# Two q tiles of batch 1 transposed by DMA instead of TensorE, with the loads of k and v of batch 2 held back and their work moved later

## The chip, the cores and the metric

The kernel runs on one core of one Trainium2 chip. The metric is device time in microseconds (us) of one execution, as the median of several runs; lower is better. The profile comes from one further execution of the same program.

## What is computed

The reference has two parts. The first is a linear attention (cosformer) over q, k and v of shape 8 batches x 8 heads x 576 rows x 64, float32. The second is a gated feed-forward layer over the 4608 rows of 512 that come out of the first.

```python
r = np.maximum(x, 0.0)                                   # phi, for q and for k
phi = np.concatenate([r * cos_w, r * sin_w], axis=-1)    # 64 -> 128 features, angle by row
kv = einsum('bhsf,bhsd->bhfd', k_p, v);  z = sum(k_p, axis=2)
num = einsum('bhsf,bhfd->bhsd', q_p, kv)
x = num / (einsum('bhsf,bhf->bhs', q_p, z)[..., None] + 1e-6)
xn = x / sqrt(mean(x*x) + 1e-6) * rms_g                  # x as 4608 x 512
out = (silu(xn @ w_gate) * (xn @ w_val)) @ w_out         # 512 -> 1536 -> 512
```

## The kernel before

**Blocks.** The output rows are worked on in nine blocks: block b holds the first 512 rows of batch b (for batch 0 another choice of 512 rows), and block 8 the 64 rows left over from each batch. They run in the order 0 to 6, 8, 7. A block has 12 gate steps (n = 0 to 11) and 4 out steps (n = 12 to 15). A gate step (`gval_step`, L869) runs four matmuls with `wg` into a psG bank and four with `wv` into a psV bank (`half_mm`, L556); then ScalarE applies silu to the first bank (`sg`, L570) and VectorE multiplies it with the second into `hT` (L571). psG and psV have two banks each, so the banks of step n are used again in step n + 2. An out step (`out_step`, L894) sums 12 matmuls of `hT` with `wo` in psC (L574); ScalarE copies the bank to `osb`, and the SP queue stores it. Block 0 has its own form of the out steps, `out_first` (L882): 48 matmuls, numbered i = 0 to 47, the first eight of each of four row tiles and then the last four of each.

**What is woven in.** While the matmuls of block b run, batch b + 1 goes through its attention. A table (`at(block, n, where, function, ...)`, L753) says in which step, and where in it, each piece is emitted: "pe" ahead of the step's matmuls, "pre" behind them, "post" at the end of the step. In `out_first` the place can also be a matmul number i. The table sets the order of the instructions on every engine by hand; each engine, and each DMA queue (SP's and GpSimd's), takes its instructions strictly in that order, and waits where an operand is not there.

The pieces of one batch are:

- `load_kv`, `load_q` (L107, L125): 1 MB each for k, v and q into one of five `raw` buffers, from SP's queue, and for the first batches from GpSimd's.
- `k_phi`, `q_phi` (L299, L317): a cosine half on VectorE and a sine half on ScalarE, from `raw` to bf16 `kp` or `qp`. `v_cast` (L369): v to bf16 `vv`.
- `q_tr_dma` (L344): tile j of q (128 rows x 1024) transposed by DMA from SP's queue into `qpT`. `q_tr_pe` with `q_tr_evac` (L359, L365): the same by eight TensorE transposes into a PSUM bank and one copy.
- `kvz_pe`, `kvz_evac` (L382, L442): the state of the batch, 72 small matmuls (40 from batch 3 on) into psA and a copy to `kvzs`. For each pair of heads all k chunks are needed, chunk 8 as the last.
- per row tile j: `nd_pe` (L446), 8 matmuls of `qpT` with `kvzs` into psA; `nd_post` (L507), the division into `xt` on VectorE; `x_sq` (L511), sum of squares on ScalarE and a power on GpSimd (`rs`, L520); `x_norm` (L523), to bf16 `xn` on VectorE; `x_tr_dma` (L539), the transposed tile by DMA from SP into `xnT`. The gate matmuls of a block read all four tiles of its `xnT` at once.

**Around the change.** For batch 1 the q tiles 0 and 1 are transposed by TensorE in steps 10 and 11 of block 0, tile 2 in `last_step` (L796) and tile 3 at i = 9 of `out_first`, each with a copy (VectorE for the first two, ScalarE for the last two). Its row tiles start (`x_first`) at `last_step`, i = 6, 11 and 19. The `xnT` tiles 0 to 2 of batch 1 go by DMA, tile 3 by TensorE at i = 43 (`x_tr`). k and v of batch 2 are loaded from GpSimd's queue in steps 8 and 10 of block 0, and worked on in the steps 14 of block 0 to 1 of block 1; its state is summed in step 3, its row tiles start in the steps 6, 8, 9 and 11 of block 1. k, v and q of batch 3 are loaded in the steps 4, 8 and 12 of block 1 (SP).

Of the kernel before, what the change touches and what calls it, by code (L numbers as in the profile page):

```python
# [10 lines left out]
BF16 = mybir.dt.bfloat16  # L11
# [6 lines left out]
def kernel(  # L18
# [17 lines left out]
    HP = H // 2  # L36
# [10 lines left out]
    V, A, G = nc.vector, nc.scalar, nc.gpsimd  # L47

    ctx.enter_context(tc.manual_schedule())
    one = ctx.enter_context(tc.tile_pool(name="one", bufs=1))  # L50
# [8 lines left out]
    psV = [ps.tile([P, 512], FP32, name=f"psV{i}") for i in range(2)]  # L59
# [10 lines left out]
    def kv_rows(src, b, hps):  # L70
        return src[b, 2 * hps[0] : 2 * hps[1], :, :].rearrange(
            "(hp hh) (s c) d -> (hh s) hp (c d)", hh=2, c=NC
        )

    def wide(b):
        return b > 2
# [4 lines left out]
    def kv_rows5(src, b, r0, r1):  # L81
        part = src[b, :, 0 : NC5 * (KP - 1), :].rearrange(
            "h (p c) d -> p h (c d)", c=NC5
        )[r0 : min(r1, KP - 1)]
        return bass.AP(part.tensor, part.offset, [[NC5 * D, r1 - r0]] + list(part.ap)[1:])
# [12 lines left out]
    def raw_kv(which, b):  # L98
        t = raw_tile(which, b)
        if wide(b):  # L100
            return t[:, :].rearrange("p (h e) -> p h e", h=H)
        return t[:, 0 : HP * NC * D].rearrange("p (hp e) -> p hp e", hp=HP)
# [4 lines left out]
    def load_kv(which, b, hps=(0, HP), eng=nc.sync):  # L107
        src = k if which == "k" else v
        if not wide(b):
            return eng.dma_start(  # L110
                out=raw_kv(which, b)[:, hps[0] : hps[1], :], in_=kv_rows(src, b, hps)
            )
        last = KP if b < B - 1 else KP - 1
        for r0, r1 in ((0, KM), (KM, last)):
            eng.dma_start(
                out=raw_kv(which, b)[r0:r1, :, :], in_=kv_rows5(src, b, r0, r1)
            )
        if last < KP:
            eng.dma_start(
                out=raw_kv(which, b)[last:KP, :, :].rearrange("p h (c d) -> p h c d", d=D),  # L120
                in_=src[b, :, S - 1 : S, :].rearrange("h s d -> s h d").unsqueeze(2)
                .to_broadcast([1, H, NC5, D]),
            )
# [25 lines left out]
    for c0, c1 in ((0, 4), (4, NC)):  # L149
        nc.sync.dma_start(  # L150
            out=raw_kv("k", 0)[:, :, c0 * D : c1 * D],
            in_=kv_rows(k, 0, (0, HP))[:, :, c0 * D : c1 * D],
# [70 lines left out]
    for i in range(3):  # L223
        m, e = math.frexp(left)
# [6 lines left out]
    def g_spread(bank, t):  # L231
# [12 lines left out]
        out=th[:, 0:NTAB], in0=fidx[:, :], scalar1=S - 1.0, scalar2=ang,  # L244
        op0=ALU.min, op1=ALU.mult,
    )
    for c0, c1, i0, less in ((0, 9, 0, 576.0), (13, 14, 13, 64.0), (19, NTAB, 13, 64.0)):
        V.tensor_scalar(
            out=th[64:128, c0:c1], in0=fidx[64:128, i0 : i0 + c1 - c0],
# [4 lines left out]
        out=th[:, NTAB : 2 * NTAB], in0=th[:, 0:NTAB], scalar1=math.pi / 2.0,  # L254
# [4 lines left out]
        out=sel[:, :, :], in_=ident[0:4, 0:4].unsqueeze(2).to_broadcast([4, NDT, P])  # L259
# [30 lines left out]
    def phi(eng, out_ap, in_ap, scale):  # L290
        if eng is A:
            A.activation(out=out_ap, in_=in_ap, func=AF.Relu, scale=scale)  # L292
        else:
            eng.tensor_scalar(  # L294
                out=out_ap, in0=in_ap, scalar1=scale, scalar2=0.0, op0=ALU.mult, op1=ALU.max
            )
# [20 lines left out]
    def q_phi(eng, b, j, part):  # L317
        o = slice(0, D) if part == 0 else slice(D, F)
        f = cos_of if part == 0 else sin_of
        phi(eng, qp_of((b, j))[:, :, o], raw_q(b)[:, :, j * D : (j + 1) * D], f(9 + j))  # L320
# [23 lines left out]
    def q_tr_dma(b, j):  # L344
        t = qp_of((b, j))
        nc.sync.dma_start_transpose(
            out=qpT[:, :, j * P : (j + 1) * P], in_=t[:, :, :].rearrange("p h f -> p (h f)")
        )
# [10 lines left out]
    def q_tr_pe(b, j, bank):  # L359
        t = qp_of((b, j))  # L360
        dst = bank.bitcast(BF16).rearrange("p (h s) -> p h s", h=H)
        for h in range(H):
            nc.tensor.transpose(dst[:, h, :], t[:, h, :], ident[:, :])  # L363

    def q_tr_evac(eng, b, j, bank):  # L365
        dst = bank.bitcast(BF16).rearrange("p (h s) -> p h s", h=H)
        copy(eng, qpT[:, :, j * P : (j + 1) * P], dst)
# [111 lines left out]
    x_of, rs_of, xn_of = {}, {}, {}  # L479
# [84 lines left out]
    def banks_of(blk, n):  # L564
        return psG[n % 2], psV[n % 2]
# [187 lines left out]
    def at(blk, n, where, f, *args):  # L753
        slots.setdefault((blk, n), {}).setdefault(where, []).append((f, args))
# [2 lines left out]
        for f, args in slots.get((blk, n), {}).get(where, []):  # L757
            f(*args)

    KCS = ((0, 1, 2), (3, 4), (5, 6), (7, 8))  # L760
    KCS5 = ((0, 1), (2,), (3,), (4,))
    for c in range(NC):
        at(0, 5 + c // 3, "post", k_phi, V, 1, c, 0)
        at(0, 5 + c // 3, "post", k_phi, A, 1, c, 1)
    for j in range(4):
        at(0, (8, 8, 9, 10)[j], "post", q_phi, V, 1, j, 0)
        at(0, (8, 9, 10, 10)[j], "post", q_phi, A, 1, j, 1)
        bank = (psC[0], psC[1], psV[0], psV[1])[j]
        if j < 2:
            at(0, 10 + j, "pe", q_tr_pe, 1, j, bank)  # L770
            at(0, 10 + j, "pre", q_tr_evac, V, 1, j, bank)
    at(0, 8, "post", load_kv, "k", 2, (0, HP), G)
    at(0, 9, "post", v_cast, G, 1, (0, 2))
    at(0, 10, "pre", v_cast, V, 1, (2, 4))
    at(0, 10, "post", load_kv, "v", 2, (0, HP), G)

    def q_tr(j, bank):
        q_tr_pe(1, j, bank)  # L780
        q_tr_evac(A, 1, j, bank)

    def x_first(j):
        nd_pe(1, j)
# [11 lines left out]
    def last_step():  # L796
        n = NNT - 1
        g, v = banks_of(0, n)
        run(0, n, "pe")
        half_mm(0, n, wg, g)  # L800
        kvz_pe(1)
        sg = four.tile([P, TB], FP32, name="sg", tag="sg")
        A.activation(out=sg[:, :], in_=g[:, 0:TB], func=AF.Silu)
        kvz_evac(A, 1)
        run(0, n, "pre")
        half_mm(0, n, wv, v)
        nd_pe(1, 0)
        q_tr(2, psV[0])
        nd_post(1, 0)
        V.tensor_tensor(out=hT[:, n, :], in0=v[:, 0:TB], in1=sg[:, :], op=ALU.mult)  # L810
        x_sq(1, 0)
        run(0, n, "post")

    for j, i in ((1, 6), (2, 11), (3, 19)):
        at(0, 12, i, x_first, j)
        at(0, 12, i, x_last, j - 1)
    at(0, 12, 9, q_tr, 3, psV[0])
    at(0, 12, 21, x_norm, 1, 3)
    at(0, 12, 21, load_q, 2)
    at(0, 12, 43, x_tr, 3, psV[0])  # L820
    for nb in range(2, B):
        b = nb - 1
        first = nb == 2
        for i, cs in enumerate(KCS5 if wide(nb) else KCS):
            kb, kn = ((0, 14), (0, 15), (1, 0), (1, 1))[i] if first else (b - 1, 12 + i)
            for c in cs:
                at(kb, kn, "post", k_phi, V, nb, c, 0)
                at(kb, kn, "post", k_phi, A, nb, c, 1)
        for i in range(2):
            vb, vn = ((0, 15), (1, 0))[i] if first else (b - 1, 13 + 2 * i)  # L830
            at(vb, vn, "post", v_cast, V, nb, (2 * i, 2 * i + 2))
        for j in range(4):
            late = j + (nb == 3)
            qb, qn = (b, 1 + j) if first else (b - (late < 2), (14 + late) % 16)
            at(qb, qn, "post", q_phi, V, nb, j, 0)
            at(qb, qn, "post", q_phi, A, nb, j, 1)
            at(qb, qn, "post", q_tr_dma, nb, j)
        kz = 3 if first else 2
        at(b, kz, "pe", kvz_pe, nb)
        at(b, kz, "pre", kvz_evac, A, nb)  # L840
        for j in range(4):
            n = ((6, 8, 9, 11) if first else (4, 6, 8, 10))[j]
            at(b, n, "mid" if n == 9 else "pe", nd_pe, nb, j)
            at(b, n, "pre", nd_post, nb, j)
            at(b, n, "post", x_sq, nb, j)
            m = n + 2 if first and j == 0 else n + 1
            at(b, m, "post", x_norm, nb, j)
            at(b, m, "post", x_tr_dma, nb, j)

    for pair in range(4):  # L850
        b = 2 * pair or 3
        at(*((2, 13), (1, 13), (3, 9), (5, 9))[pair], "post", load_q_tails, pair)
        at(b, 3, "post", q_tails_phi, V, pair, 0)
        at(b, 3, "post", q_tails_phi, A, pair, 1)
        at(b, 3, "post", q_tails_tr_dma, pair)
        at(b, 12, "pe", nd_tails_pe, pair)
        at(b, 12, "pre", nd_post, 2 * pair + 1, 4)
        at(b, 12, "post", x_sq, 2 * pair + 1, 4)
        at(b, 13, "post", x_norm, 2 * pair + 1, 4)
        at(b, 13, "post", x_tr_dma, 2 * pair + 1, 4)  # L860
    for nb in range(3, B):
        b = nb - 2
        for which, n in zip("kvq", {1: (4, 8, 12), 2: (3, 5, 8)}.get(b, (0, 3, 6))):
            if which == "q":
                at(b, n, "post", load_q, nb)
            else:
                at(b, n, "post", load_kv, which, nb)
# [91 lines left out]
```

## Time and profile before

| | |
|---|---|
| median of 3 runs | 323.44 us (323.1 to 324.34) |
| profiled execution | 322.91 us |
| its span in the profile | 321.1 us |
| TensorE (PE) busy | 313.6 us, 98% |
| VectorE (DVE) busy | 185.4 us, 58% |
| ScalarE (ACT) busy | 165.8 us, 52% |
| GpSimd (POOL) busy | 40.5 us, 13% |
| bytes moved by DMA | 53.76 MB |

The profiled execution's own time lies 1.8 us above its span, and 0.5 us below the median of the runs. In the timeline a row gives start and length in us, engine, line, operation, the tiles, and how many instructions are merged; in brackets stands the idle time of the engine just before, and what ended it. SPq rows are DMA issues on SP's queue: their length is the time of issuing, not of the transfer. In the chain of waits a row gives start, length and the instruction on the path that ended last. The granted clock is full in all 40 slices.

### The profile page before, as it was taken

How to read it: one execution, taken by the hardware profiler on the slowest of the kernel's cores; microseconds unless marked ns; L12 is line 12 of the kernel's file. 1: busy time of each engine (PE TensorE's matmuls, PEld its weight loads, DVE VectorE, ACT ScalarE, POOL GpSimd, SP SyncE). 2: the span in 40 equal slices, each digit the busy share in tenths (PEclk: the TensorE clock that was granted, in tenths of full speed). 3: DMA queues.
4: the chain of work that ended last, by engine and by line, in shares of the span. 5: the costliest groups of instructions: out<-in, count | busy, mean ns of one | idle time of the engine just before them, and what ended most of it. 6: DMA issues, size and time to landing. Idle time of an engine off the chain costs nothing.

```text
span 321.1 us, 6023 instructions
## 1 busy us (share of the span) xinstructions
PE 313.6 (98%) x2274; PEld 162.4 (51%) x2310; DVE 185.4 (58%) x382; ACT 165.8 (52%) x322; POOL 40.5 (13%) x79
## 2 busy tenths in 40 slices
PE   7999999999999999999999999999999999999996
PEld 2689564544454445444544445544544444444444
DVE  7976977668457773777457644781676034204410
ACT  5766756754574466554744575446543233223321
POOL 9771211002001100010001100100011000000000
PEclk9999999999999999999999999999999999999999
DMA  7999999788999999999799959995522500041002
GB/s 232 239 270 269 282 329 227 201 183 190 223 226 211 187 263 187 221 247 182 162 186 230 197 163 200 197 217 163 99 59 41 116 33 0 0 102 31 1 35 98
DMA packets 80092, 53.76 MB, mean 167 GB/s; under 512 B 52235, under 2 KB 74047, under 8 KB 80063
## 3 DMA queue, kind: packets, MB, share of 16 engines
q1 hardware_dynamic: 73110, 41.25, 62.1%
q0 software_dynamic: 6944, 12.13, 15.5%
q8 instruction: 18, 0.29, 0.4%
q14 instruction: 12, 0.09, 0.1%
q10 hardware_dynamic: 8, 0.00, 0.0%
HBM read 37.83 MB, written 9.44 MB: 147 GB/s over the span
## 4 chain that ended last, share of the span: by engine, by line
PE 94%; DMA 2%; DVE 1%; issue 1%; POOL 1%; ACT 0%; POOLq 0%; ACTq 0%
PE psC L574 27%; PE psV L556 27%; PE psG L556 26%; PE psV L643 2%; PE psA L449 2%; DMA vv<-in_v_dram 2%; PE psG L574 2%; PE psG L643 2%; PE psA L387 2%; PE psA L394 1%; PE psA L474 0%; PE psV L363 0%; PE psG L430 0%; PE psC L546 0%; POOL raw L135 0%
## 5 line engine op out<-in xcount | busy, mean ns | idle before, releaser
L571 DVE TENSOR_TENSOR hT<-psV,sg 128x512 bf16<-128x512 f32 x99 | 68.2, 689 | 96.5 <-PE psV L556 64.1
L556 PE MATMUL psV<-xnT,wv 128*128 128x512 bf16 x344 | 89.6, 379 | 0.7 <-issue 0.2
L570 ACT ACTIVATE sg<-psG 128x512 f32<-128x512 f32 x99 | 58.6, 592 | 60.8 <-PE psG L556 52.7
L556 PE MATMUL psG<-xnT,wg 128*128 128x512 bf16 x337 | 88.5, 379 | 0.7 <-issue 0.2
L574 PE MATMUL psC<-wo,hT 128*128 128x512 bf16 (+1 forms) x400 | 88.4, 376 | 0.4
L574 PEld LDWEIGHTS <-hT 128*128 128x128 bf16 x456 | 43.1, 98 | 47.7
L556 PEld LDWEIGHTS <-wv 128*128 128x128 bf16 x400 | 39.0, 98 | 46.8
L556 PEld LDWEIGHTS <-wg 128*128 128x128 bf16 x400 | 37.0, 98 | 39.9 <-DVE xnT L288 0.2
L520 POOL TENSOR_TENSOR rs<-ms,mhalf 128x1 f32<-128x1 f32 x36 | 20.5, 570 | 193.9 <-ACT scr L515 193.7
L286 ACT COPY osb<-psC 128x512 f32<-128x512 f32 x32 | 18.7, 585 | 49.9 <-PE psC L574 46.1
L515 ACT ACTIVATE scr<-xt 128x513 bf16<-128x513 f32 x36 | 22.8, 635 | 23.3 <-DVE xt L499 22.3
L527 DVE SCALAR_TENSOR_TENSOR xn<-xt,rs,gb 128x512 bf16<-128x512 f32 (+1 forms) x37 | 26.9, 730 | 9.9 <-POOL rs L520 9.9
L292 ACT ACTIVATE kp<-raw,tab 128x256 bf16<-128x256 f32 (+2 forms) x51 | 28.8, 607 | 2.4 <-DMA raw<-in_k_dram 2.4
L499 DVE TENSOR_TENSOR xt<-psA,rec 128x512 f32<-128x512 f32 x36 | 24.9, 691 | 1.2
L292 ACT ACTIVATE qp<-raw,tab 128x512 bf16<-128x512 f32 (+1 forms) x36 | 23.3, 666 | 1.2 <-DMA raw<-in_q_dram 1.1
L294 DVE TENSOR_SCALAR kp<-raw,tab 128x256 bf16<-128x256 f32 (+2 forms) x53 | 20.1, 428 | 0.5 <-DMA raw<-in_k_dram 0.5
L294 DVE TENSOR_SCALAR qp<-raw,tab 128x512 bf16<-128x512 f32 (+1 forms) x34 | 15.3, 463 | 4.7 <-DMA raw<-in_q_dram 4.7
L449 PEld LDWEIGHTS <-qpT 128*128 128x128 bf16 x224 | 10.6, 97 | 6.6
L556 PE MATMUL psV<-xnT_tail,wv 128*128 128x512 bf16 x48 | 12.3, 379 | 0.1
L556 PE MATMUL psG<-xnT_tail,wg 128*128 128x512 bf16 x46 | 12.0, 379 | 0.1
L288 DVE CAST vv<-raw 116x1280 bf16<-116x1280 f32 (+1 forms) x13 | 11.1, 857 | 1.3 <-DMA raw<-in_v_dram 1.3
L449 PE MATMUL psA<-kvzs,qpT 128*128 128x65 bf16 x224 | 11.4, 193 | 0.0
(102 smaller groups left out, 177.7 us busy)
## 6 DMA issues: line engine op xcount, KB each, us to landing
out_dram<-osb SPq DMA_DIRECT2D x27, 256.0 KB, 2.3
raw<-in_q_dram SPq DMA_DIRECT2D x6, 1024.0 KB, 9.1
raw<-in_k_dram SPq DMA_DIRECT2D x5, 1120.0 KB, 8.8
raw<-in_v_dram SPq DMA_DIRECT2D x5, 1120.0 KB, 9.4
raw<-in_k_dram POOLq DMA_DIRECT2D x2, 1152.0 KB, 19.2
raw<-in_v_dram POOLq DMA_DIRECT2D x2, 1152.0 KB, 15.7
out_dram<-osb SPq DMA_DIRECT2D x17, 128.0 KB, 2.6
wg<-in_moe_w_gate_dram POOLq DMA_DIRECT2D x3, 512.0 KB, 13.8
```

The costliest lines, as they stand in the source:

```text
L286: A.copy(out=o, in_=i)
L292: A.activation(out=out_ap, in_=in_ap, func=AF.Relu, scale=scale)
L294: eng.tensor_scalar(out=out_ap, in0=in_ap, scalar1=scale, scalar2=0.0, op0=ALU.mult, op1=ALU.max)
L449: nc.tensor.matmul(heads[:, g, hp, :], lhsT=qpT[:, h, j * P : (j + 1) * P], rhs=kvzs[b][:, g, hp * E : (hp + 1) * E], start=True, stop=True,)
L499: V.tensor_tensor(out=xt[:, 0:DM].rearrange("p (hp g d) -> p g hp d", g=2, d=D), in0=heads[:, :, :, 0:D], in1=rec[:, :, :].unsqueeze(3).to ...
L515: A.activation(out=scr[:, :], in_=xt[:, 0 : DM + 1], func=AF.Square, scale=1.0 / math.sqrt(DM), accum_out=ms[:, :],)
L520: G.tensor_tensor(out=rs[:, :], in0=ms[:, :], in1=mhalf[:, :], op=ALU.pow)
L527: V.scalar_tensor_tensor(out=xn_of[(b, j)][:, c], in0=x_of[(b, j)][:, c], scalar=rs_of[(b, j)][:, :], in1=gb[:, c], op0=ALU.mult, op1=ALU. ...
L556: nc.tensor.matmul(bank[:, cols[0] : cols[1]], lhsT=w[:, t, n * P : (n + 1) * P], rhs=x[:, t, cols[0] : cols[1]], start=(t == 0), stop=(t ...
L570: A.activation(out=sg[:, :], in_=g[:, 0:TB], func=AF.Silu)
L571: V.tensor_tensor(out=hT[:, n, :], in0=v[:, 0:TB], in1=sg[:, :], op=ALU.mult)
L574: nc.tensor.matmul(bank[:, 0 : cols[1] - cols[0]], lhsT=hT[:, n, j * P : (j + 1) * P], rhs=wo[:, n, cols[0] : cols[1]], start=(n == 0), st ...
```

## The change

Tiles 2 and 3 of q of batch 1 are no longer transposed by TensorE, but by DMA from SP's queue (`q_last`), with their VectorE halves of `q_phi` moved into `last_step`. The row tiles 2 and 3 of batch 1 start at i = 22 and 28 of `out_first`. The loads of k and v of batch 2 leave the steps 8 and 10 of block 0; GpSimd now issues them behind a one-element copy of the last `xn` tile of batch 1 (`load_held`), and the load of q of batch 2 moves ahead to i = 7. Work on k of batch 2 moves to the steps 3 to 7 of block 1, in groups of two chunks, its `v_cast` to the steps 5 and 6 and to GpSimd, its state to step 8, its row tiles to the steps 9, 10, 12 and 13, with norm and transpose one step behind each. The loads of k, v and q of batch 3 move to the steps 8, 10 and 14 of block 1, `q_phi` of batch 3 by one step to the steps 0 to 3 of block 2, and the loads of the q rows left over (batches 2 and 3) by two steps. A one-row piece of the loads of k and v of batch 7 moves from SP's queue to GpSimd's.

```diff
         if last < KP:
-            eng.dma_start(
+            G.dma_start(
...
-    KCS = ((0, 1, 2), (3, 4), (5, 6), (7, 8))
+    KCS2 = ((0, 1), (2, 3), (4, 5), (6, 7), (8,))
...
-        at(0, (8, 8, 9, 10)[j], "post", q_phi, V, 1, j, 0)
+        if j < 2:
+            at(0, 8, "post", q_phi, V, 1, j, 0)
...
-    at(0, 8, "post", load_kv, "k", 2, (0, HP), G)
-    at(0, 10, "post", load_kv, "v", 2, (0, HP), G)
-    def q_tr(j, bank):
-        q_tr_pe(1, j, bank)
-        q_tr_evac(A, 1, j, bank)
+    def q_last(j):
+        q_phi(V, 1, j, 0)
+        q_tr_dma(1, j)
+
+    def load_held(b, key):
+        hold = one.tile([1, 1], BF16, name="hold")
+        G.tensor_copy(out=hold[:, :], in_=xn_of[key][0:1, 0:1])
+        load_kv("k", b, eng=G)
+        load_kv("v", b, eng=G)
...
         nd_pe(1, 0)
-        q_tr(2, psV[0])
+        q_last(2)
+        q_last(3)
         nd_post(1, 0)
...
-    for j, i in ((1, 6), (2, 11), (3, 19)):
+    for j, i in ((1, 6), (2, 22), (3, 28)):
         at(0, 12, i, x_first, j)
         at(0, 12, i, x_last, j - 1)
-    at(0, 12, 9, q_tr, 3, psV[0])
-    at(0, 12, 21, x_norm, 1, 3)
-    at(0, 12, 21, load_q, 2)
-    at(0, 12, 43, x_tr, 3, psV[0])
+    at(0, 12, 7, load_q, 2)
+    at(0, 12, 29, x_norm, 1, 3)
+    at(0, 12, 29, load_held, 2, (1, 3))
+    at(0, 12, 44, x_tr, 3, psV[0])
...
-        for i, cs in enumerate(KCS5 if wide(nb) else KCS):
-            kb, kn = ((0, 14), (0, 15), (1, 0), (1, 1))[i] if first else (b - 1, 12 + i)
+        for i, cs in enumerate(KCS5 if wide(nb) else KCS2):
+            kb, kn = (1, 3 + i) if first else (b - 1, 12 + i)
...
-            vb, vn = ((0, 15), (1, 0))[i] if first else (b - 1, 13 + 2 * i)
-            at(vb, vn, "post", v_cast, V, nb, (2 * i, 2 * i + 2))
+            vb, vn = (1, 5 + i) if first else (b - 1, 13 + 2 * i)
+            at(vb, vn, "post", v_cast, G if first else V, nb, (2 * i, 2 * i + 2))
...
-            late = j + (nb == 3)
-            qb, qn = (b, 1 + j) if first else (b - (late < 2), (14 + late) % 16)
+            late = j + 2 * (nb == 3)
+            qb, qn = (b, j) if first else (b - (late < 2), (14 + late) % 16)
...
-            at(qb, qn, "post", q_tr_dma, nb, j)
-        kz = 3 if first else 2
+            at(qb, 3 if first else qn, "post", q_tr_dma, nb, j)
+        kz = 8 if first else 2
...
-            n = ((6, 8, 9, 11) if first else (4, 6, 8, 10))[j]
-            at(b, n, "mid" if n == 9 else "pe", nd_pe, nb, j)
+            n = ((9, 10, 12, 13) if first else (4, 6, 8, 10))[j]
+            at(b, n, "pe", nd_pe, nb, j)
...
-            m = n + 2 if first and j == 0 else n + 1
-            at(b, m, "post", x_norm, nb, j)
-            at(b, m, "post", x_tr_dma, nb, j)
+            at(b, n + 1, "post", x_norm, nb, j)
+            at(b, n + 1, "post", x_tr_dma, nb, j)
...
-        at(*((2, 13), (1, 13), (3, 9), (5, 9))[pair], "post", load_q_tails, pair)
+        at(*((2, 13), (1, 15), (3, 9), (5, 9))[pair], "post", load_q_tails, pair)
...
-        for which, n in zip("kvq", {1: (4, 8, 12), 2: (3, 5, 8)}.get(b, (0, 3, 6))):
+        for which, n in zip("kvq", {1: (8, 10, 14), 2: (3, 5, 8)}.get(b, (0, 3, 6))):
```

## Prediction

> **What bounds the kernel now.** I read the page first (busy times, chain), then the chain of waits around the ends of blocks 0 and 1, then the timelines of VectorE and of SP's queue there.
>
> ```profile
> PE 313.6 (98%) x2274; PEld 162.4 (51%) x2310; DVE 185.4 (58%) x382; ACT 165.8 (52%) x322; POOL 40.5 (13%) x79
> ...
> PE 94%; DMA 2%; DVE 1%; issue 1%; POOL 1%; ACT 0%; POOLq 0%; ACTq 0%
> ```
>
> TensorE is the bound: 94% of the chain, and its 7.5 us of idle time lie almost all ahead of the first units. So an edit saves time only by taking matmuls off TensorE, and it costs time wherever TensorE has to wait for something it now finds ready.
>
> The chain at the end of block 0 (start, length, what):
>
> ```profile
> 42.04 0.45 PE psV L363 x8
> 42.49 1.29 PE psG L574 x6
> ...
> 44.68 0.45 PE psV L363 x8
> ...
> 47.52 0.24 PE psA L449 x8
> ...
> 54.25 0.22 PE psG L556
> ```
>
> A q tile costs TensorE 0.45 us (eight transposes, L363), an out matmul 0.215 (1.29 / 6), a row tile 0.24 (L449). Block 1 starts at 54.25, block 2 at 87.68: 33.43 us, with no gap over 0.2.
>
> SP's queue and VectorE at the end of block 1:
>
> ```profile
> 73.14 1.21 SPq L540 DMA_TRANSPOSE xnT<-xn  x1
> 74.45 1.02 SPq L115 DMA_DIRECT2D raw<-in_v_dram  x2
> ...
> 81.02 1.21 SPq L540 DMA_TRANSPOSE xnT<-xn  x1
> 82.33 0.53 SPq L126 DMA_DIRECT2D raw<-in_q_dram  x1
> ...
> 90.39 6.26 SPq L346 DMA_TRANSPOSE qpT<-qp  x4
> ```
>
> ```profile
> 82.60 0.83 DVE L288 CAST vv<-raw 116x1280 bf16<-116x1280 f32 x1 [1.27 <-DMA raw<-in_v_dram]
> ...
> 89.65 0.49 DVE L294 TENSOR_SCALAR qp<-raw,tab 128x512 bf16<-128x512 f32 x1 [4.69 <-DMA raw<-in_q_dram]
> ```
>
> Loads and transposes leave SP in one order: v of batch 3 goes right behind the transpose of batch 2's tile 0, q right behind that of tile 3. VectorE waits for both loads already, v 8.15 us after issue (74.45 to 82.60), q 7.32 (82.33 to 89.65). Today neither wait reaches TensorE. This margin is what the change spends.
>
> **Step 1: the two q tiles.** Removed from TensorE: 2 x 0.45 = **0.90 us**, on the path. Their ScalarE copies (about 1.0 each) were covered. Added: two DMA transposes on SP, issued near 40.5 and 41.8, since their VectorE halves (0.48 each) fit into the 1.36 us VectorE idles at 42.15. Landing of such a tile: 3.0 to 7.9, median 3.2 us. Tile 2 is needed at i = 22, near 47.1, tile 3 at i = 28, near 48.6: covered, even at 6 us.
>
> The Trainium skill prices this otherwise: "TensorE: Matmul & The Clock Gate", Part 4: PE-mode transpose, gives about 275 ns for a 128x128 transpose inside a kernel. By that the 16 would free 4.4 us, an estimate, and the sum below would end 3.5 us lower; the row here has 8 in 0.45 us, 56 ns each, and decides.
>
> **Step 2: the start of block 1.** With 0.45 us less behind it, i = 0 starts at 42.04. Then row tile 2 starts at 42.04 + 22 x 0.215 + 0.24 = 47.0, row tile 3 at 48.6 (47.52 before). From the start of a row tile to the end of its norm the trace has 3.66 us (47.52 to 51.18), a pure chain over VectorE, ScalarE, GpSimd, VectorE. For tile 3 that gives 52.4; TensorE arrives at i = 44 at 52.3 and transposes it. The four matmuls behind put block 1 at 53.7 at the earliest: of the 0.90, 0.55 is left.
>
> But the gate matmuls also need tile 2 of `xnT` by DMA. Its norm waits on VectorE behind the division of tile 3 and ends near 50.9; before, its transpose was issued at 49.6 and block 1 came 4.6 us later. Now 2.8 us are left. Landings of such tiles: 2.5 to 9.5, median 4.3. And the load of q of batch 2 (1 MB) is now ahead of it on SP (near 46.9, behind tile 0's transpose) instead of behind. Where a q load was ahead by 2 us (106.14, then 108.48), the transpose took 8.4; there a v load was in flight too, here not. I take 4.1, nearest the median: block 1 at 55.0, so **+0.75** against 54.25, the 0.90 included. Bounds: -0.55 (landing 2.8) and +2.7 (landing 6.0).
>
> **Step 3: the state of batch 2.** Chunk 8 of k is now worked on at the end of step 7, the state starts step 8. VectorE's product of a step starts 0.11 us after TensorE has gone on (62.64 against 62.53) and occupies 0.60; chunk 8 adds 0.3, and about 0.2 passes until TensorE reads it: 1.2 us. The 72 matmuls take 1.27, and the 17th needs chunk 8, after 0.28. TensorE waits **+0.9 to 1.0**; I take 1.0 (0.7 to 1.2). Before, step 2 lay between.
>
> The held loads themselves: GpSimd waits for the norm of tile 3 (52.4) and issues k and v by 54.3. Nothing is queued behind that wait but its own casts. k is needed near T + 7.6 (T: start of block 1), v near T + 11. The trace has 12.4 to 20.9 us for GpSimd's loads, all with others queued ahead, and 6.0 for a q load on SP. With two in a pause I take 7 and 11: k has 9 us, v 12, and psV's second bank gives two steps more. Cost nothing; if the 20.9 held, k would be 10 us late.
>
> A row of the Trainium skill, "DMA: Bandwidth & Descriptors", Anatomy of one DMA, puts such a load at 2.0 us plus its bytes at 436 GB/s. That is 4.7 us for k, an estimate; no run here shows these loads alone, and by it they would be early.
>
> **Step 4: the end of block 1.** Due, with step 3's microsecond in it:
> - product of step 10: T + 11 x 1.73 + 1.43 (state and its gap) + 2 x 0.24 + 1.0 + 0.11 = T + 22.05;
> - norm of tile 0 0.60 behind it, its DMA 0.78 after that (72.36 to 73.14), v's load 1.31 later (73.14 to 74.45): T + 24.7, where it was T + 20.2;
> - v landed 8.15 later: T + 32.9. In VectorE's order the first `v_cast` of batch 3 (step 13) now stands **ahead of** the norm of tile 3 (step 14; before step 12, ahead of the cast). So this norm starts at T + 33.6, and its transpose X = T + 34.4.
>
> Block 2 is due at T + 33.43 + 1.0 = T + 34.4, the moment of that issue. At the shortest landing, 2.5 or 2.6, it starts 2.6 us late.
>
> q of batch 3 follows X by 1.31, is there 7.32 later, its tile 0 goes out 0.74 after that (89.65 to 90.39) and lands 3.2 later (the median; that very one took 4.5): X + 12.6. The row tile that reads it was due 8.13 after block 2's start (87.68 to 95.81): X + 8.15. This wait overtakes the first one: **+4.4**. Bounds: +2.6 (block 2's own wait alone), +7.5 (q in 9.1, its median, and 4.5). From step 4 of block 2 on, everything depends on its own block again, as before.
>
> **Free:** the casts on GpSimd (1.15 each, idle there; POOL is at 13%), the tails' load (3.4 to 7.9 for two steps more than 8 us), and the one-row loads of batch 7 (1.8 us off SP, about 1 us each on GpSimd, which idles 15 us there; TensorE has no gap).
>
> **Sum:** 0.75 + 1.0 + 4.4 = +6.15 us. On the profiled execution's 322.91 (span 321.1 and 1.8 around it) that is 329.1; the median of the runs, 323.44, lies 0.5 above it, so **329.6**. All low bounds give +2.75, all high ones +11.4.
>
> **Rivals.**
> - *Shorter waits, still slower.* The same places, with q there in 6.0 as it once was and the transpose of step 2 in 2.8: -0.55 + 1.0 + 3.0 = +3.4, 326.9. For it: the loads now have fewer neighbours. Against: v took 8.15 with little beside it.
> - *Not slower.* One mechanism: loads in a queue that carries nothing else land at the rate that DMA reached around 45 us (about 400 GB/s): 1.16 MB in 2.9 us, plus about 2 (a finished tile's store lands in 2.3), 5 us. Place: the `v_cast` ahead of tile 3's norm. It decides from 5 us down: v is then there at T + 29.7, before that norm's own operands (about T + 31), and q comes 3 us sooner. Then block 2 has some 0.7 left, and -0.55 + 1.0 + 0.7 = +1.15: 324.6. Against it: DMA was 81% busy at some 200 GB/s during v's load.
> - *k or v late.* GpSimd's loads keep 15 to 20 us: VectorE and ScalarE hold up steps 5 to 8 by 3 us or more, +9 to +12: 333 to 335. For it: all their rows are long. Against: all had other loads queued ahead.
> - *The change gains its 0.90 and no wait appears:* 322.5. Faster by over 0.5% (1.6 us, about what a measurement of this kernel can tell from no change) isn't to be had from 0.9 us; it would take something I do not see.
>
> **Chances.** Forecast (+4 to +9) 0.60; shorter waits (+1.6 to +4) 0.22; not slower, or the bare gain (within 1.6) 0.11; late k or v (over +9) 0.04; faster 0.03. So slower 0.86, same 0.11, faster 0.03. The range reaches into the third and leaves out the rest on each side, +1.2 to +9.2: 324.6 to 332.6.
>
> **What would show it.** In the profile after: no L363 behind 42 us, two L346 issues near 41; block 1 starting at 54 to 56, with TensorE idle until DMA `xnT`; an idle TensorE of 1 us at `kvz_pe` of batch 2, released by `kp`; a `vv` cast of VectorE with some 3 us of DMA wait ahead of the last norm of batch 2; block 2 starting late by 2.6 or more; and a wait for `qpT` or `sg` in its first steps. Wrong would be: block 2 starting on time, or the `vv` wait gone.

## The result, and the profile after

The changed kernel takes **328.56 us** (median of 6 runs, 327.57 to 329.33), the kernel before 323.46 (6 runs on the same chip, 323.1 to 324.34). The ratio is 1.0151, with a 95% interval of 1.0129 to 1.0173: 5.1 us slower, where 329.6 was forecast.

The page of the profile after, its span, busy times, clock row and the shares of the chain of work that ended last:

```profile
span 326.8 us, 5994 instructions
...
PE 316.3 (97%) x2258; PEld 162.1 (50%) x2294; DVE 185.0 (57%) x380; ACT 163.6 (50%) x320; POOL 43.9 (13%) x84
...
PEclk9999999999979999999999999999999999999999
...
PE 88%; DMA 5%; DVE 3%; issue 1%; POOL 1%; ACT 1%; SPq 0%; ACTq 0%; DVEq 0%; POOLq 0%
```

TensorE still bounds the kernel. Two things are new. The share of the chain that is DMA has grown from 2% to 5%, and one of the 40 slices has a granted clock below 9 tenths: the twelfth, from 89.9 to 98.0 us, which holds the start of block 2.

The waits of TensorE (microseconds in total, number of waits, the longest):

```profile
PE psG L556 <- DMA xnT<-xn: 2.4, 1, 2.4
...
PE psA L394 <- DVE kp L294: 0.7, 1, 0.7
```

Neither was there before. The chain of waits shows where they stand (start, length, what):

```profile
40.24 1.27 PE psA L394 x72
...
54.55 0.86 PE psG L556 x4
...
69.25 0.27 DVE kp L294
69.66 1.08 PE psA L394 x56
...
79.97 7.49 DMA raw<-in_v_dram
88.29 0.74 DVE xn L527
89.06 2.41 DMA xnT<-xn
91.61 1.54 PE psG L556 x4
93.15 1.71 PE psV L556 x4
94.86 1.19 PE psG L556 x4
96.04 0.86 PE psV L556 x4
...
101.59 0.24 PE psA L449 x8
```

The same chain in the kernel before, at the state of batch 1, the start of block 2 and the first row tile of batch 3:

```profile
39.56 1.27 PE psA L394 x72
...
87.68 0.86 PE psG L556 x4
...
95.81 0.25 PE psA L449 x8
```

Block 1 starts at 54.55. The state of batch 2 (`psA L394`) waits for VectorE's last product of k. Block 2 starts at 91.61, released by a transpose of `xn`, which stands behind a norm, which stands behind the cast of a `v` that landed late. Its first three groups of four matmuls then take 1.54, 1.71 and 1.19 us; the fourth takes 0.86, as all of them did before. So the time is lost in these stretches, each from one event on TensorE to the next:

| stretch ends with | before | after | difference |
|---|---|---|---|
| state of batch 1 | 39.56 | 40.24 | +0.68 |
| start of block 1 | 54.25 (14.69) | 54.55 (14.31) | -0.38 |
| start of block 2 | 87.68 (33.43) | 91.61 (37.06) | +3.63 |
| first row tile of batch 3 | 95.81 (8.13) | 101.59 (9.98) | +1.85 |
| end of the span | 321.1 (225.3) | 326.8 (225.2) | -0.1 |

The +0.68 is there by 10.5 us: the first load of v landed 0.7 later, before anything that the change touches, and other runs below have 39.9 here. Without it the rows add up to 5.0; the medians differ by 5.1. The +3.63 parts into 1.08 (step 8 of block 1 goes on at 70.90, due at 69.82) and 2.55 (block 2, due at 54.55 + 33.43 + 1.08 = 89.06, starts at 91.61).

SP's queue of the kernel after, where block 1 ends:

```profile
78.08 1.20 SPq L540 DMA_TRANSPOSE xnT<-xn  x1
79.38 1.02 SPq L115 DMA_DIRECT2D raw<-in_v_dram  x2
...
89.06 1.20 SPq L540 DMA_TRANSPOSE xnT<-xn  x1
90.31 0.57 SPq L126 DMA_DIRECT2D raw<-in_q_dram  x1
97.63 6.88 SPq L346 DMA_TRANSPOSE qpT<-qp  x4
```

VectorE's rows that belong to it, with the idle time ahead of a row and what ended it:

```profile
87.55 0.83 DVE L288 CAST vv<-raw 116x1280 bf16<-116x1280 f32 x1 [3.34 <-DMA raw<-in_v_dram]
88.29 0.74 DVE L527 SCALAR_TENSOR_TENSOR xn<-xt,rs,gb 128x512 bf16<-128x512 f32 x1
...
96.88 0.49 DVE L294 TENSOR_SCALAR qp<-raw,tab 128x512 bf16<-128x512 f32 x1 [1.22 <-DMA raw<-in_q_dram]
```

v goes out at 79.38 (74.45 before). VectorE waits 3.34 us for it, and the norm runs in the same moment that the cast leaves the engine. The transpose goes out at 89.06, exactly when block 2 is due.

### The profile page after: what moved, and what is told of

The parts are those of the page before. It is cut to its first block, busy times and chain, and to the rows that moved or that the text cites. A ratio compares the mean times of both kernels' runs of the same rounds, so it can differ in the third digit from the quotient of the medians.

```text
span 326.8 us, 5994 instructions
## 1 busy us (share of the span) xinstructions
PE 316.3 (97%) x2258; PEld 162.1 (50%) x2294; DVE 185.0 (57%) x380; ACT 163.6 (50%) x320; POOL 43.9 (13%) x84
## 4 chain that ended last, share of the span: by engine, by line
PE 88%; DMA 5%; DVE 3%; issue 1%; POOL 1%; ACT 1%; SPq 0%; ACTq 0%; DVEq 0%; POOLq 0%
PE psV L556 27%; PE psG L556 26%; PE psC L574 22%; DMA raw<-in_v_dram 2%; DMA vv<-in_v_dram 2%; PE psV L643 2%; PE psA L449 2%; PE psG L643 2%; PE psA L387 2%; PE psG L574 1%; DVE xn L527 1%; DMA xnT<-xn 1%; PE psA L394 1%; DVE xt L499 1%; PE psA L474 0%
## 5 line engine op out<-in xcount | busy, mean ns | idle before, releaser
L556 PE MATMUL psG<-xnT,wg 128*128 128x512 bf16 x339 | 89.5, 382 | 3.0 <-DMA xnT<-xn 2.4
L520 POOL TENSOR_TENSOR rs<-ms,mhalf 128x1 f32<-128x1 f32 x36 | 19.8, 551 | 183.8 <-ACT scr L515 183.5
L294 DVE TENSOR_SCALAR kp<-raw,tab 128x256 bf16<-128x256 f32 (+2 forms) x53 | 21.2, 444 | 0.8 <-DMA raw<-in_k_dram 0.8
L288 DVE CAST vv<-raw 116x1280 bf16<-116x1280 f32 (+1 forms) x11 | 9.4, 856 | 3.3 <-DMA raw<-in_v_dram 3.3
```

What stands on the lines that cost most here:

```text
L294: eng.tensor_scalar(out=out_ap, in0=in_ap, scalar1=scale, scalar2=0.0, op0=ALU.mult, op1=ALU.max)
L520: G.tensor_tensor(out=rs[:, :], in0=ms[:, :], in1=mhalf[:, :], op=ALU.pow)
L556: nc.tensor.matmul(bank[:, cols[0] : cols[1]], lhsT=w[:, t, n * P : (n + 1) * P], rhs=x[:, t, cols[0] : cols[1]], start=(t == 0), stop=(t ...
```

## The experiments

**What each lost microsecond is.** Theory: three waits follow from three places (the late v with a norm behind its cast, the late last chunk of k, and the clock that falls in the idle time), and each can be taken away by itself. Rival: a shared cause, DMA load, makes all of them.

*The cast behind the norm.*

```diff
+            if nb == 3:
+                vn = 14 + i
             at(vb, vn, "post", v_cast, G if first else V, nb, (2 * i, 2 * i + 2))
```

> The changed kernel with one thing else: the first cast of v of batch 3 stands behind the norm of batch 2's tile 3 on VectorE (steps 14 and 15 instead of 13 and 15). v's load stays as late as it is. Theory (the order on VectorE makes block 2 late): the norm starts when its own operands are there, near 85.9 instead of 88.3, block 2 waits 0.3 us or less instead of 2.4, the granted clock stays at 1.0 there, and the q load goes out 2.4 us earlier; its chain to the first row tile of batch 3 may still hold TensorE for 1 to 2 us. Time 325.4 to 326.2 against 328.6. Rival A (a late v holds TensorE by itself, through the state of batch 3): 328 to 329. Rival B (q's chain costs nothing): the whole 4.4 us of the stage goes, 324.2.

Measured: 329.37, ratio 1.0177 (1.0138 to 1.0216), no gain at all; the expectation failed. VectorE, then SP's queue in this run:

```profile
85.55 0.75 DVE L527 SCALAR_TENSOR_TENSOR xn<-xt,rs,gb 128x512 bf16<-128x512 f32 x1 [1.69 <-POOL rs L520]
```

```profile
86.88 0.33 SPq L585 DMA_DIRECT2D out_dram<-osb  x1
87.31 1.21 SPq L540 DMA_TRANSPOSE xnT<-xn  x1
```

The chain of waits of the same run:

```profile
87.31 4.53 DMA xnT<-xn
91.98 1.86 PE psG L556 x4
```

The norm runs 2.7 us sooner, as it should. But its transpose stands on SP behind a store and goes out only at 87.31, and then takes 4.53 us instead of 2.41: stores and transposes (0.8 MB) pass in one burst from 87.25 to 89.8, after v has landed at 87.2. So the late v can hold block 2 in two ways, through VectorE's order and through the queue behind it; the next run tests the second. The first had been thought to be the only one.

*v off SP's queue as well* (the edit above, and this):

```diff
-                at(b, n, "post", load_kv, which, nb)
+                eng = G if (which, nb) == ("v", 3) else nc.sync
+                at(b, n, "post", load_kv, which, nb, (0, HP), eng)
```

> As with the cast behind the norm, and v of batch 3 loaded from GpSimd's queue (issued near 78, as late as before) instead of SP's. With the cast alone moved the norm was 2.7 us earlier, but its transpose landed 4.5 us after issue: 0.8 MB of stores and transposes stood behind v on SP's queue until 89.8. Theory (SP's queue behind v is the second thing that holds block 2): the stores now go out as they come, the transpose lands 2.4 to 3 us after its issue near 87, block 2 starts 0.5 to 1.5 us late, the clock stays at 1.0; 326 to 327.2. Rival (v's bytes hold the transpose on whatever queue they travel, since they share the same DMA engines): landing 4 us or more, block 2 over 2.5 us late, 328 or above.

Measured: 326.97, ratio 1.0118 (1.0102 to 1.0133). With VectorE and SP both free of v, the last transpose lands 2.8 us after its issue instead of 4.5, and the wait at the start of block 2 falls from 3.2 to 1.4 us. v itself is hardly sooner: its first cast starts at 86.72 (87.29 with the cast moved alone). A wait for `qpT` of 1.6 comes out from behind. The second cause is shown.

*v's load one step sooner.* `{1: (8, 10, 14)` becomes `{1: (8, 9, 14)`.

> The changed kernel with one thing else: on SP's queue v of batch 3 is loaded ahead of the transpose of batch 2's tile 0 (step 9 instead of 10), so it goes out right behind k, near 70 instead of 79.4. Order on VectorE unchanged. Theory (cast ahead of the norm, and v late for it): v lands by 82, the cast waits for nothing, block 2 waits 0.3 us or less; the same time as with the cast behind the norm, 325.4 to 326.2. Rival A (the transposes of batch 2 now sit behind v on SP's queue and land late): block 2 still waits 1 us or more, 327 or above. Rival B (q's chain costs nothing): 324.2.

Measured: 326.55, ratio 1.0099 (1.0082 to 1.0115), 2.0 us below the change, between the forecast and its rival A. The waits of TensorE:

```profile
PE psA L449 <- DMA qpT<-qp: 1.8, 1, 1.8
...
PE psG L556 <- DMA xnT<-xn: 1.0, 1, 1.0
```

The clock stays at 1.0 throughout. Block 2 waits 1.0 instead of 2.4 (0.3 or less was expected), and again the q of batch 3 is late next: issued at 87.84, its transpose at 95.05, which lands 4.13 later.

*TensorE kept busy while it waits.* Eleven matmuls on zeros, whose result nobody reads, ahead of block 2:

```diff
+    at(2, 0, "pe", filler, 11, psC[0])
```

> The changed kernel with eleven extra matmuls of zeros (0.215 us each, 2.4 us) into a free psC bank between block 1 and block 2, where TensorE idles 2.44 us. They add work that the output doesn't use. Theory (the first three groups of block 2 take 1.54, 1.71 and 1.39 us instead of 0.86 to 1.03 because the idle stretch lowers the granted clock): the clock stays at 1.0 there, the groups take 0.86 each, and 1.86 us go, less what q's chain then takes back (its first row tile can't come before about 100.8, due 99.7): 326.7 to 327.8. Rival (the clock falls for another reason, or the slow groups are something else): 328.5 or above.

Measured: 327.59, ratio 1.013 (1.011 to 1.0151), as expected. The start of block 2 in the kernel after, by windows (the stretch and its length; busy time and count of PE, PEld, DVE, ACT and POOL; granted clock, DMA share, GB/s). An instruction that reaches over the edge of a window is counted on both sides of it.

```profile
90.00:91.00 1.00, 0.00 (x0) 0.00 (x0) 0.57 (x1) 0.41 (x1) 0.00 (x0) 1.00 0.67 131
...
92.00:93.00 1.00, 1.00 (x4) 0.36 (x3) 0.00 (x0) 0.00 (x0) 0.00 (x0) 0.50 0.51 122
...
94.00:95.00 1.00, 1.00 (x4) 0.30 (x2) 0.03 (x1) 0.00 (x0) 0.00 (x0) 0.50 1.02 329
...
96.00:97.00 1.00, 1.00 (x14) 0.55 (x12) 0.12 (x1) 0.12 (x1) 0.00 (x0) 1.00 1.21 328
```

With the filler:

```profile
92.00:94.00 2.00, 2.00 (x11) 0.88 (x9) 0.69 (x1) 0.60 (x1) 0.00 (x0) 1.00 0.99 328
```

Without it TensorE idles, then runs at half clock until 95.4, where a group of four matmuls takes 1.71 us; with it the clock stays full and a group takes 0.86. What comes out now is a wait for `qpT`:

```profile
PE psA L449 <- DMA qpT<-qp: 0.7, 1, 0.7
```

So the clock costs 1.85 us on the trace, and 1.0 net (328.56 less 327.59): the wait for q, 0.7 here, takes back most of the rest. The change's own runs say the same: five had a mean granted clock of 0.995 (median 328.62), one had 1.0 and took 327.57.

*The last chunk of k one step sooner.*

```diff
-    KCS2 = ((0, 1), (2, 3), (4, 5), (6, 7), (8,))
+    KCS2 = ((0, 1), (2, 3), (4, 5), (6, 7, 8))
```

> The changed kernel with one thing else: chunk 8 of k of batch 2 is worked on with chunks 6 and 7 in step 6, not alone in step 7. Theory (the state waits for VectorE's chunk 8): the wait of 0.7 us at the state's 17th matmul and the 1.08 us that step 8 comes late go; 327.5 to 327.7 against 328.6. Rival (GpSimd's casts of v, which end at 68.25, hold the state instead): the wait stays, 328.3 or above.

Measured: 327.35, ratio 1.0121 (1.0098 to 1.0144). The number is near the forecast (327.5 to 327.7), but not for the forecast's reason: step 8 is still 0.88 late (1.08 in the change). In the change, VectorE and GpSimd have these rows:

```profile
64.47 0.61 DVE L294 TENSOR_SCALAR kp<-raw,tab 128x256 bf16<-128x256 f32 x2
...
65.75 1.50 DVE L294 TENSOR_SCALAR kp<-raw,tab 128x256 bf16<-128x256 f32 x2
```

```profile
65.83 2.42 POOL L288 CAST vv<-raw 128x1152 bf16<-128x1152 f32 x2 [10.74 <-PE psG L556]
```

A pair of k takes 0.61 us of VectorE alone, and 1.50 beside GpSimd's casts of v. Those casts are a part of the change (both stood on VectorE before) and now run just ahead of the state. VectorE with the chunk moved:

```profile
65.26 2.47 DVE L294 TENSOR_SCALAR kp<-raw,tab 128x256 bf16<-128x256 f32 x2
...
68.24 0.86 DVE L294 TENSOR_SCALAR kp<-raw,tab 128x256 bf16<-128x256 f32 x3
```

Here the pair beside the casts takes 2.47, and the products of chunks 6, 7 and 8 come together at 68.24, when the state has begun (67.93). So moving one chunk by one step doesn't heal the wait, as the products ahead of it are slow. Step 8 gives 0.2 of the 1.2 us gained; the rest goes with the clock, whose mean was 0.999 in three of the four runs, but no run tried this apart.

**Why the q tiles land in time.** Theory: the k and v loads of batch 2 need not be held for their own sake; unheld they cost the q tiles nothing. Rival: side by side, the transposes starve.

```diff
+    at(0, 8, "post", load_kv, "k", 2, (0, HP), G)
     at(0, 9, "post", v_cast, G, 1, (0, 2))
     at(0, 10, "pre", v_cast, V, 1, (2, 4))
+    at(0, 10, "post", load_kv, "v", 2, (0, HP), G)
...
-        load_kv("k", b, eng=G)
-        load_kv("v", b, eng=G)
```

> The changed kernel with one thing else: k and v of batch 2 are loaded by GpSimd in the steps 8 and 10 of block 0 again, as before; the one-element copy stays, without loads behind it. Theory (the q tiles of batch 1 have 5 us of room by DMA, so the loads need not be held): block 1 starts no later than in the changed kernel by more than 0.5 us, k and v of batch 2 are early, and the late steps of block 1 stay as they are: 328 to 329 against 328.6. Rival (the pause is needed): the q tiles and xn tiles land behind 2.3 MB on GpSimd's queue, TensorE waits for qpT or xnT at the start of block 1 for 1 us or more: 329.6 or above.

Measured: 334.32, ratio 1.0347 (1.0327 to 1.0367). The theory fell. The chain, and the longest of TensorE's waits:

```profile
40.59 12.99 DMA qpT<-qp
```

```profile
PE psA L449 <- DMA qpT<-qp: 6.7, 2, 6.0
```

The two tiles land 12.4 and 13.0 us after their issue, against 4.5 and 5.1 in the change. The DMA queues from 46 to 48 us (packets, MB, share of time), q0 GpSimd's, q1 SP's:

```profile
q0 software_dynamic: 159, 0.71, 93.4%
q1 hardware_dynamic: 159, 0.04, 9.1%
```

The same view of the change, from 44 to 46 us:

```profile
q1 hardware_dynamic: 1386, 0.35, 89.8%
q0 software_dynamic: 21, 0.02, 5.5%
```

Both queues get through the same number of packets, 159 each; but a packet of GpSimd's load is 4.5 KB and one of the transpose 0.25 KB. The Trainium skill, "DMA: Bandwidth & Descriptors", Queues, rings and completion order, says that each DMA engine takes turns between the queues that have work, a whole packet at a time. The trace agrees, with 159 against 159. But these turns are only a part of the 13 us. From 40 to 44 us SP's queue moves no packet at all (in the change it begins between 42 and 44), and from 50 on, with 22 of GpSimd's packets left, the tiles still need over 3 us. What holds them there was not tried.

*k and v of batch 2 from SP, in their old steps, instead of from GpSimd.*

> As with the loads not held, but k and v of batch 2 go out from SP's queue at the end of k's work of batch 1 (near 34), not from GpSimd's. There the q tiles landed 12.4 and 13.0 us after issue, at 53 to 54, and between 46 and 48 us the two queues moved 159 packets each: 0.71 MB for GpSimd, 0.04 MB for SP. Theory (the queues take turns packet by packet, so SP's 256-byte packets get a small share while GpSimd's 4.5-KB packets are there): with the loads on SP's own queue in 2.3-KB packets the transposes come behind them in order; they land when k and v are through, near 48 to 50, TensorE waits 1 to 3 us instead of 6; 329.5 to 332. Rival (all the bytes of k, v and the weights have to pass first, on whatever queue): landing at 53 as there, 333.5 to 335.

Measured: 335.23, ratio 1.0368 (1.0344 to 1.0391). It didn't test what it was for. A step says only what stands ahead on the engine; SP had nothing to wait for and sent k off at 8.98 and v at 15.47, among the weights; TensorE then waits 3.5 us for `wv`, and the state of batch 1 comes at 45.64 instead of 40. The q tiles land in 5.8 and 6.2 us, although GpSimd's queue is busy ahead of them too: from 46 to 48 us it moves 417 packets of about 1 KB, and SP's none. So other traffic on GpSimd's queue does not by itself cost 13 us; with the loads of k and v in it, in the run before, it did. Whether their bytes or the size of their packets made the difference stays open.

*The two tiles on TensorE again, everything else as changed.*

```diff
     def q_last(j):
         q_phi(V, 1, j, 0)
-        q_tr_dma(1, j)
+        if j == 2:
+            q_back(j)
+
+    def q_back(j):
+        q_tr_pe(1, j, psV[0])
+        q_tr_evac(A, 1, j, psV[0])
...
+    at(0, 12, 9, q_back, 3)
```

> The changed kernel with the two q tiles of batch 1 transposed by TensorE again (tile 2 in the last step of block 0, tile 3 at i = 9, copies on ScalarE), all else as in the change. Theory (0.45 us of TensorE each, ahead of row tile 2, from which the chain to the start of block 1 hangs): 0.9 us more, 329.2 to 329.7 against 328.6. Rival (the wait for the last norm ahead of block 1 has slack, or the copies on ScalarE delay the chain): no difference, or 1.5 us and more.

Measured: 329.95, ratio 1.0196 (1.0176 to 1.0215), 1.4 above the change and a little above the forecast. Each tile takes 0.45 us of TensorE again (42.36 and 44.99), and from the state of batch 1 to block 1 pass 15.98 us instead of 14.31. That is more than the 0.90 of the tiles. Block 1 also waits 0.9 us here for the transpose of row tile 2; in the change it does not:

```profile
52.04 3.68 DMA xnT<-xn
```

So the part of the change that moves these tiles gains, and the time is lost by what makes room for it.

**Whether the loss can be undone.** If the account is complete, taking away all of its causes must bring the 5.1 us back, and the 0.9 of the tiles should show, in part at least.

*All loads of batch 3 by step 9, and the norm of tile 3 of batch 2 a step sooner.*

```diff
-            at(b, n, "post", x_sq, nb, j)
-            at(b, n + 1, "post", x_norm, nb, j)
-            at(b, n + 1, "post", x_tr_dma, nb, j)
+            early = first and j == 3
+            m = n if early else n + 1
+            at(b, n, "pre" if early else "post", x_sq, nb, j)
+            at(b, m, "post", x_norm, nb, j)
+            at(b, m, "post", x_tr_dma, nb, j)
...
-        for which, n in zip("kvq", {1: (8, 10, 14), 2: (3, 5, 8)}.get(b, (0, 3, 6))):
+        for which, n in zip("kvq", {1: (8, 9, 9), 2: (3, 5, 8)}.get(b, (0, 3, 6))):
```

> The changed kernel with k, v and q of batch 3 loaded in one go (steps 8, 9, 9), all ahead of the transposes of batch 2, and with tile 3 of batch 2 squared ahead of the copy to osb in step 13 and normed in step 13. Theory (order of loads and norm is all that makes the end of block 1 late): block 2 starts on time, q is there before its step, no wait for qpT, clock 1.0; the 4.4 us of this stage go: 324.0 to 324.8. Rival (three loads in a row make 3.3 MB and hold up the transposes of batch 2 or the stores, or q's chain keeps a part): 325.5 or above.

Measured: 323.86, ratio 1.0031 (1.0016 to 1.0046), a little better than expected. Nearly all of the loss is back by the order of the loads and one norm; the two were not tried apart. The wait for k (0.7) is left.

*The same, with k in three steps of three chunks and the row tiles of batch 1 sooner.*

```diff
-    KCS2 = ((0, 1), (2, 3), (4, 5), (6, 7), (8,))
+    KCS2 = ((0, 1, 2), (3, 4, 5), (6, 7, 8))
...
-    for j, i in ((1, 6), (2, 22), (3, 28)):
+    for j, i in ((1, 6), (2, 20), (3, 25)):
...
-    at(0, 12, 29, x_norm, 1, 3)
-    at(0, 12, 29, load_held, 2, (1, 3))
+    at(0, 12, 26, x_norm, 1, 3)
+    at(0, 12, 26, load_held, 2, (1, 3))
```

> As the one before, and chunks of k of batch 2 in three groups in the steps 3 to 5, so ahead of GpSimd's casts of v, and the row tiles 2 and 3 of batch 1 started at i = 20 and 25. Theory: the state of batch 2 waits for nothing (1.08 us go) and block 1 starts 0.2 to 0.3 earlier; with the 4.4 of the stage behind gone too, what is left is the gain of the two q tiles: 322.6 to 323.2, against 323.5 of the kernel before. Rival (the state then waits for GpSimd's casts, or VectorE and ScalarE fall behind in the steps 3 to 5): 323.8 or above.

Measured: 324.33, ratio 1.004 (1.0026 to 1.0053); the expectation failed. The state no longer waits (`psA L394 x72` in one piece of 1.27 us). But block 2 waits 1.4 for a transpose that went out at 84.57 and took 3.8: the 3.3 MB of k, v and q of batch 3 pass on SP's queue until about 84, and the transposes and stores that stand behind them until 88.

*The same, with q of batch 3 at step 13:* `(8, 9, 13)`.

> As the version with all repairs, but q of batch 3 is loaded right behind the transpose of batch 2's tile 3 (step 13), not together with k and v. There block 2 still waited 1.4 us: that transpose, issued at 84.6, landed 3.8 us later, with k, v, q, two transposes and two stores ahead of it. Theory (q's 1 MB in this queue is what holds it): the transpose goes out by 84 and lands within 2.7 us, block 2 waits 0.2 us or less; q's chain to the first row tile of batch 3 then keeps 0.2 to 1.0 us: 323.0 to 323.9, against 323.3 of the kernel before. Rival (k and v alone fill the queue that long): the wait at block 2 stays over 1 us and q's chain adds its own, 324.5 or above.

Measured: 327.39, ratio 1.0114 (1.0089 to 1.0139); failed again, on the other side. Block 2 starts without a wait, and then its first row tile waits for q:

```profile
PE psA L449 <- DMA qpT<-qp: 2.3, 1, 2.3
```

q went out at 86.32, landed 6.63 later, its transpose took another 4.65, and the clock fell again, behind this wait. That is the prediction's chain of q in the open.

*Between the two:* `(8, 9, 11)`.

> As the version with all repairs, but q of batch 3 is loaded behind the transpose of batch 2's tile 1 (step 11): later than with k and v, earlier than behind tile 3's. Theory (both earlier places fail by about 1 to 2 us, on opposite sides): q lands near 86, the transpose of tile 3 within 3 us of its issue near 84, block 2 waits 0.5 us or less, q's chain nothing: 323.0 to 323.7, against 323.3 of the kernel before. Rival (the bytes of k, v and q of batch 3 between 67 and 88 us are simply too many, wherever q stands): block 2 waits 1 us or more, 324.2 or above.

Measured: **323.33** (11 runs, 322.96 to 323.94) against 323.21 for the kernel before (15 runs), ratio 1.0002 (0.9993 to 1.0012): no difference. Its span is 321.5, and only one of the waits is left, at the start of block 2:

```profile
PE psG L556 <- DMA xnT<-xn: 0.4, 1, 0.4
```

From the state of batch 1 to block 1 it takes 14.24 us (14.69 before). So half of the 0.90 arrives there, and the wait of 0.4 at block 2 takes it away again; the other half is lost on the way to block 1. The loss is explained and undone; no version found is faster than the kernel before.

## Why the prediction was right: its steps, one by one

**Step 1, the q tiles.** Right in size: 0.45 us each, on both sides of the comparison (before, and with the tiles back on TensorE). The 275 ns that the Trainium skill, "TensorE: Matmul & The Clock Gate", Part 4: PE-mode transpose, gives for one transpose did not show as a cost: one transpose has 219 ns in the trace, but they overlap, and eight took 0.45 again, 56 ns each. The cover held, with landings of 4.5 and 5.1. But it held only because the loads were held back. The bounds of 3.0 to 7.9 came from tiles with other neighbours, and with the loads not held it was 13.0.

**Step 2, the start of block 1.** Mis-sized: +0.75 forecast, -0.38 measured. The term is the landing of tile 2's `xnT`, taken as 4.1 us. It went out at 51.65 and was there by 54.55, 2.9 at most. The q load 4.1 us ahead of it on SP (47.57) did not hold up block 1. Nor is the landing of 4.1 us far off: with the two tiles back on TensorE the same transpose took 3.7 and held block 1 by 0.9. What remained was the step's other limit, the last norm and its transpose on TensorE, which gives back 0.52 of the 0.90.

**Step 3, the state of batch 2.** Right in size, 1.08 for 1.0, and by the chain that was forecast, with chunk 8 behind the product of its step: TensorE leaves step 7 at 68.37, chunk 8 starts at 69.17 and the state goes on at 69.66, 1.3 us where 1.2 was forecast. What the forecast did not see is that VectorE's rows slow beside GpSimd's casts, which it listed as free. That costs 0.1 here at most, and it is why moving the chunk alone won only 0.2. The held loads were free, as forecast: k landed after 8.3 us (7 taken) and v after 11.3 (11 taken). The estimate of 4.7 for k, from the Trainium skill, "DMA: Bandwidth & Descriptors", Anatomy of one DMA, is too short here, with eight stores on SP's queue beside it; the trace has 8.3.

**Step 4, the end of block 1.** The total is right, and its parts are not. Forecast: 2.6 for block 2's own wait, then the chain of q, together 4.4. Measured: 2.55, then 1.85 of half clock, together 4.40. The transpose was forecast at 54.55 + 34.4 = 88.95 and went out at 89.06. Two things were wrong. The forecast named VectorE's order as what holds the norm, and the queue behind v would have held block 2 by itself. And it did not see the clock. The chain of q is real, but it lay behind the slowed matmuls: q's transpose was issued at 97.63 and its row tile came at 101.59 without a wait. It shows at 0.7 when the clock is held up, at 1.8 and 2.3 when block 2 starts sooner. That the sum came out is then no accident of the first part, but it is one of the second.

**The sum.** Forecast 0.75 + 1.0 + 4.4 = 6.15, measured -0.38 + 1.08 + 4.40 = 5.10. Nearly the whole miss is step 2.

**The rivals.** The not-slower case asked for loads that land in 5 us; v took about 8. The late k and v did not come, as GpSimd's queue had nothing ahead of them. That the bare 0.90 is gained was not seen in any run; the nearest, with everything repaired, ends level with before.

## What to carry to other kernels

A few tenths of a microsecond taken off the bounding engine are worth having only if every load that makes room for them still lands ahead of its own consumer: for each load sent later, list what stands behind it on its queue and behind its first reader on that reader's engine, for either alone is enough to hold the next stage. Keep transposes by DMA, with their small packets, away from another queue's large ones, and hold a load back by a true dependency, since a late place in the program holds nothing where the issuing engine has nothing to wait for. A wait is dearer than its length if the bounding engine's clock falls in it.

## What was not expected of the hardware

**The clock falls after a short wait.** An idle time of 2.4 us on TensorE was followed by 3.4 us at a granted clock of 0.50 (91.97 to 95.38, by the granted clock of the windows); five of the change's six runs have the mean clock that goes with it, 0.995. With the cast behind the norm, 3.2 us of idle time and 6.8 at half clock (90.9 to 97.7) stand together. Idle times of 2.4 (tiles back on TensorE), 2.3 (q at step 13) and 2.2 us (k and v from SP) were each followed by 3.4 us at half clock, and one of 2.3, with the last chunk sooner, by none in the profiled execution. The Trainium skill, "TensorE: Matmul & The Clock Gate", Part 1: The HAM clock gate, says that the clock is halved after at least one idle window of about 3.4 us, in windows that run free of the kernel. The half clock and the chance in it agree with the trace; the length of the idle time does not, as 2.2 us were enough. Why is left open: no run varied the idle time by itself.

**Packets take turns, bytes do not.** 159 packets each for two queues within 2 us were 0.71 MB for the one and 0.04 MB for the other. In that run transposes that had landed in 5 us took 12 to 13; the equal turns show from 45 to 48 us only.

**VectorE slows beside GpSimd's casts.** Two products of k took 0.61 us alone, and 1.50 and 2.47 beside a cast on GpSimd. Which resource they share was not tried.
